# Three sets of sixteen small loads in SyncE's queue of a one-core decode block

## The chip, the cores and the metric

The kernel runs on one core of one Trainium2 chip. The metric is the device time of one launch in microseconds. Several runs are taken and their median is given; the profile is of one further execution, with the trace's clock.

## The reference

A decode step for four sequences (B = 4, one token each, D = 512). The normalized input feeds two branches whose results are added to the input:

```python
xn = layernorm(x)
out = x + A(xn, k_cache, v_cache, wq, wo) + B(xn, w1, w2, w3, w4)

# A: attention of one query against a cache, 32 heads, 4096 positions, head size 128
q = (xn @ wq) as (B, 32, 1, 128)
p = softmax(q @ k_cache^T * 128 ** -0.5)
a = (p @ v_cache) as (B, 1, 4096) @ wo

# B: a shift along the sequence, which for one token leaves only zeros, then an MLP
x1 = xn + 0
b = x1 + gelu(layernorm(x1) @ w3) @ w4
```

All is float32. `k_cache` and `v_cache` are 4 x 32 x 4096 x 128, 268 MB each. `wq` and `wo` have 8.4 MB each, `w3` and `w4` 3.7 MB each.

## The kernel before

The 128 pairs of a sequence and a head are taken in 32 groups of four (`G = 4`). For a group, keys and values are each one load of 128 partitions with 64 KB a partition, 8.4 MB. There are two key buffers (`ks`) and one value buffer (`vs`).

- VectorE loops over the groups (L320 to L337). It multiplies the keys with the query in two halves (L329), sums each product over the head size (L330), and takes the maximum (L335 to L337). After each half it raises `summed`; after the second, the key buffer is free.
- ScalarE takes the exponentials (L348) and copies results out of PSUM (L353, L355); with the last it raises `done`, and the value buffer is free.
- TensorE waits for the values (`landed`), multiplies them with the exponentials (L382), and sums over partitions (L387, L389).
- SyncE issues the loads in an order written out by hand, all through the helper `load` (its instructions have line L165) and all in one queue, q1 in the profile. First come `wq`, `w3` and the keys of group 0, then the keys of group 1, the values of group 0, and the keys of group 2 in two halves. Then, for j from 0 to 29: a wait for `summed` of group j and the keys of group j + 2 (from j = 1 on), and a wait for `done` of group j and the values of group j + 1. The last group's values go into a key buffer, and `w4` into the value buffer.
- The output weight `wo` follows in seven pieces (L288 and L292), into the last key buffer once VectorE is through with it. The first piece has half of the 32 blocks; the next have 8, 4, 2 and 1; the last block is cut in two halves. Each piece has its own semaphore (`wo_sems`), and TensorE takes up the blocks piece by piece (L419, L151, and L434 for the last block).
- The result of 4 x 512 is stored in two halves, the first by SyncE and the second by ScalarE (L441). After its store SyncE raises `bye`, on which GpSimd clears the semaphores, and SyncE waits for both stores.

The input x comes in on ScalarE's queue, q10 in the profile.

Of the kernel before, what the change touches and what calls it, by code (L numbers as in the profile page):

```python
# [88 lines left out]
def decode_block(ctx: ExitStack, tc: tile.TileContext, x, k, v, wq, wo, w3, w4, out):  # L89
    nc = tc.nc  # L90
# [14 lines left out]
    def sb(name, *shape):  # L105
        return nc.alloc_sbuf_tensor(name, [P, *shape], F32).ap()

    def bank(name):
        return nc.alloc_psum_tensor(name, [P, 4 * DH], F32).ap()
# [21 lines left out]
    rz = sb("rz", G * NJ)  # L131
    ot = sb("ot", G * NJ)

    total = bank("total")[:, 0:P]
    y = bank("y")
    pv = bank("pv")
# [7 lines left out]
    def rows(flat, j):  # L144
        n = G * S * DH
        return flat[j * n:(j + 1) * n].rearrange("(p n) -> p n", p=P)

    def blocks4(start, stop, w, m, src):
# [6 lines left out]
    wo_sems = [nc.alloc_semaphore(f"wo{n}") for n in range(7)]  # L155
    sems = {n: nc.alloc_semaphore(n) for n in (
        "x", "w3", "wq", "k0", "k1", "landed", "last", "w4", "go", "pv", "copied", "poz",
        "half0", "half1", "nm", "dve", "summed", "expd", "done", "bye", "out")}
    wo_sb = ks[LAST % 2].rearrange("p (c n) -> p c n", c=WC)
    wo_cuts = ((0, 16), (16, 24), (24, 28), (28, 30), (30, WC - 1))  # L160
    w4_sb = vs[:, :NF * D].rearrange("p (m n) -> p m n", m=NF)
    g4 = vs[:, NF * D:NF * D + 4 * 32].rearrange("p (m i) -> p m i", m=4)

    def load(o, i, sem, by, *after, queue="SP"):
        return do(queue, lambda e: e.dma_start(o, i), *after, done=(sems[sem], 16, by))  # L165
# [22 lines left out]
        out=ident, in_=ident, compare_op=ALU.not_equal, fill=1.0, base=0, pattern=[[-1, P]],  # L188
# [64 lines left out]
    for c in range(NC):  # L253
        for t in range(4):
# [22 lines left out]
    parts = [load(ks[0][:, n:n + HALF], rows(kf, 2)[:, n:n + HALF], f"half{i}", 16, (sems["summed"], i + 1))  # L277
             for i, n in enumerate((0, HALF))]
    for j in range(LAST - 1):
        if j > 0:  # L280
            load(ks[j % 2], rows(kf, j + 2), f"k{j % 2}", None, SUMMED[j])
        load(vs, rows(vf, j + 1), "landed", None, DONE[j])
# [3 lines left out]
    wo_r = wo.rearrange("(p c) n -> p c n", c=WC)  # L286
    for (c0, c1), sem in zip(wo_cuts, wo_sems):
        nc.sync.dma_start(wo_sb[:, c0:c1], wo_r[:, c0:c1]).then_inc(sem, 16)  # L288
    half = D // 2
    for n, sem in enumerate(wo_sems[-2:]):  # L290
        n *= half
        nc.sync.dma_start(wo_sb[:, WC - 1, n:n + half], wo_r[:, WC - 1, n:n + half]).then_inc(sem, 16)  # L292

    def take(engine, sem, n=1):

        engine.wait_ge(sems[sem], n)
        engine.sem_inc(sems[sem], -n)  # L297
# [11 lines left out]
    with nc.Fori(0, NJ // 2, engines=OrderedEngineSet([DVE]), head_slot={DVE: 192}) as j:  # L309
        e, n = nc.vector, 0  # L310
# [8 lines left out]
        for s in range(2):  # L319
# [14 lines left out]
            rm, nm = small[:, s, 0:1], small[:, s, 1:2]  # L334
# [68 lines left out]
    for m in range(NF):  # L403
        t, g, n = (m, g4[:, m, :], 32) if m < 4 else (m % 4, gT[:, m, :], B)
# [26 lines left out]
    for t in range(4):  # L431
# [7 lines left out]
        if t % 2:  # L439
            q = slice(P * (t - 1), P * (t + 1))  # L440
            stored = do("SP" if t < 2 else "ACT", lambda e: e.dma_start(out.rearrange("b s d -> (b s) d")[:, q], row[:, q]),  # L441
                        *moved.values(), done=(sems["out"], 16, 8 * t + 8))

    nc.sync.sem_inc(sems["bye"], 1)
    nc.scalar.sem_inc(sems["bye"], 1)
    nc.gpsimd.wait_ge(sems["bye"], 2)
# [31 lines left out]
```

## Time and profile before

| | |
|---|---|
| median of 3 runs | 1302.76 us (1302.56 to 1303.01) |
| profiled execution: span from first to last instruction | 1301.5 us; no separate time is given for this execution |
| median less this span | 1.26 us |
| TensorE matmul busy | 368.7 us (28%) |
| TensorE weight load busy | 132.8 us (10%) |
| VectorE busy | 1164.4 us (89%) |
| ScalarE busy | 93.5 us (7%) |
| GpSimd busy | 2.5 us (0%) |
| TensorE clock granted, mean | 0.622 |
| HBM read | 561.00 MB, 431 GB/s over the span |

Busy shares are taken over the whole span. In a window or a queue's line, the "share of 16 engines" is the time of that queue's packets, divided by sixteen times the length of the window; a packet is put down to the window in which it starts, so that a short window can show more than 100%. A load is one data packet for each row and, on each transfer engine that it uses, one short packet that raises the semaphore, which is called its completion here. The time "to landing" runs from the issue to the last completion.

### The profile page before, as it was taken

The page shows a single profiled execution, that of the slowest core. Times are in us where ns is not written, and L with a number is a line of the kernel's source. Part 1 is how long each engine was busy: PE and PEld are TensorE (multiplying, and loading weights), DVE is VectorE, ACT ScalarE, POOL GpSimd, SP SyncE. Part 2 cuts the span into 40 slices and gives each one's busy share as a digit, 9 for nine tenths or more (in the row PEclk, how much of TensorE's full clock was granted, in tenths as well). Part 3 has the DMA queues.
Part 4 walks back from the last instruction along what each step waited for, and adds up shares of the span by engine and source line. Part 5 has one row for each costly group of instructions (what it writes and reads, how often), then busy time and mean ns, then how long its engine had stood idle before and what let it go on. Part 6 is the DMA issues. An engine that isn't in the chain of part 4 may idle for free. (4 is left out here: it accounts for less than half of the span.)

```text
span 1301.5 us, 6687 instructions
## 1 busy us (share of the span) xinstructions
PE 368.7 (28%) x2652; PEld 132.8 (10%) x2652; DVE 1164.4 (89%) x323; ACT 93.5 (7%) x332; POOL 2.5 (0%) x14
## 2 busy tenths in 40 slices
PE   4121332321233321133331133332123332123337
PEld 2000111100011100011110011110011110001112
DVE  2599999999999999999999999999999999999990
ACT  0100000000000000000000000000000000000001
POOL 0000000000000000000000000000000000000000
PEclk9555666655666655666655566665566665566668
DMA  9999999999999999999999999999999999999998
GB/s 404 448 421 449 423 441 427 435 435 425 443 423 447 423 447 421 441 429 431 439 421 447 423 447 423 445 423 437 433 425 445 421 447 423 447 423 443 425 426 367
DMA packets 10830, 561.08 MB, mean 431 GB/s; under 512 B 1212, under 2 KB 1476, under 8 KB 1736
## 3 DMA queue, kind: packets, MB, share of 16 engines
q1 hardware_dynamic: 10808, 561.00, 99.7%
q8 instruction: 3, 0.05, 0.0%
q14 instruction: 3, 0.02, 0.0%
q10 hardware_dynamic: 16, 0.01, 0.0%
HBM read 561.00 MB, written 0.01 MB: 431 GB/s over the span
## 5 line engine op out<-in xcount | busy, mean ns | idle before, releaser
L329 DVE TENSOR_TENSOR ks<-ks,qb 128x8192 f32<-128x8192 f32 x64 | 556.3, 8692 | 63.7 <-DVEq L297 58.7
L330 DVE TENSOR_REDUCE sc<-ks 128x64 f32<-128x8192 f32 x64 | 555.9, 8686 | 2.2
L382 PE MATMUL pv<-vs,pw 128*32 128x512 f32 x1984 | 286.9, 743 | 874.9 <-PEq L297 874.9
L382 PEld LDWEIGHTS pv<-vs,pw 128*32 128x32 f32 x1984 | 79.2, 133 | 1057.9 <-issue 1057.9
L353 ACT COPY os<-pv 128x512 f32<-128x512 f32 x32 | 18.7, 585 | 827.8 <-ACTq L297 827.8
L348 ACT ACTIVATE pw<-sc,small 32x128 f32<-32x128 f32 x128 | 50.9, 398 | 278.1 <-ACTq L297 276.9
L387 PE MATMUL poz<-sel,os 128*128 128x4 f32 x256 | 32.8, 252 | 28.0 <-PEq L297 28.0
L387 PEld LDWEIGHTS poz<-sel,os 128*128 128x128 f32 x256 | 31.0, 191 | 56.1 <-issue 56.1
L348 ACT ACTIVATION_READ_ACCUMULATOR pw<-sc,small 32x1 f32 x128 | 23.5, 184 | 0.0
L436 DVE COPY os<-total 4x128 f32<-4x128 f32 x2 | 0.6, 282 | 16.2 <-PE total L434 16.2
L335 DVE TENSOR_REDUCE small<-sc 128x1 f32<-128x128 f32 x32 | 9.2, 286 | 4.7
L363 DVE RECIPROCAL rz<-oz 128x96 f32<-128x96 f32 (+1 forms) x2 | 1.1, 552 | 12.6 <-ACT oz L355 12.5
L389 PE MATMUL poz<-rs,ones 128*128 128x4 f32 x64 | 11.7, 253 | 0.0
L245 DVE STREAM_TRANSPOSE vs<-pw 128x1024 f32<-128x1024 f32 x1 | 1.2, 1245 | 10.9 <-ACT pw L244 10.9
L321 DVE STREAM_TRANSPOSE qb<-qg 128x128 f32<-128x128 f32 x32 | 10.0, 312 | 1.1
L202 DVE TENSOR_REDUCE lns<-vs 4x1 f32<-4x512 f32 x1 | 0.7, 674 | 11.3 <-DMA vs<-in_A_x_dram 11.3
L320 DVE COPY qg<-qT 128x4 f32 x32 | 5.4, 170 | 4.9 <-issue 4.9
L389 PEld LDWEIGHTS poz<-rs,ones 128*128 128x128 f32 x64 | 9.7, 192 | 0.0
L215 PE MATMUL pt<-vs,pw 4*128 4x4 f32 x16 | 4.0, 372 | 18.1 <-DVE pw L209 18.1
L419 PE MATMUL y<-ks,X 128*4 128x512 f32 x48 | 8.0, 835 | 3.5 <-DMA ks<-in_A_wo_dram 3.5
L355 ACT COPY oz<-poz 128x8 f32 x32 | 5.3, 165 | 50.8 <-ACTq L297 50.8
L382 PE MATMUL pv<-ks,pw 128*32 128x512 f32 x64 | 8.5, 692 | 0.0
(75 smaller groups left out, 74.8 us busy)
## 6 DMA issues: line engine op xcount, KB each, us to landing
ks<-in_A_k_cache_dram SPq DMA_DIRECT2D x2, 4096.0 KB, 26.9
vs<-in_B_w_dram SPq DMA_DIRECT2D x2, 3584.0 KB, 23.1
ks<-in_A_wo_dram SPq DMA_DIRECT2D x1, 4096.0 KB, 21.9
ks<-in_A_wo_dram SPq DMA_DIRECT2D x1, 2048.0 KB, 26.5
ks<-in_A_wo_dram SPq DMA_DIRECT2D x1, 1024.0 KB, 28.6
ks<-in_A_wo_dram SPq DMA_DIRECT2D x1, 512.0 KB, 29.4
ks<-in_A_k_cache_dram SPq DMA_DIRECT2D x31, 42.2
vs<-in_A_v_cache_dram SPq DMA_DIRECT2D x31, 26.8
```

The costliest lines, as they stand in the source:

```text
L320: step(e.tensor_copy(qg, pairs[:, s, bass.ds(j, 1)].rearrange("p o n -> p (o n)")))
L321: step(e.transpose(qb.rearrange("p (n m) -> p n m", m=HP), qg.unsqueeze(2).to_broadcast([P, DH // HP, HP])))
L329: step(e.tensor_tensor(out=kt, in0=kt, in1=qb.unsqueeze(1).to_broadcast([P, w, DH]), op=ALU.mult))
L330: step(e.reduce_sum(sc[s][:, c:c + w], kt, axis=AX.X))
L335: step(e.reduce_max(rm, sc[s], axis=AX.X))
L348: i = nc.scalar.activation(pw[hp, :, 4 * h:4 * h + 4], sc[s][hp, :].rearrange("p (g w) -> p g w", w=4), AF.Exp, bias=small[hp, s, 1:2], sc ...
L353: nc.scalar.copy(os, pv.rearrange("p (m d) -> p m d", m=4)).then_inc(sems["copied"], 1)
L355: nc.scalar.copy(ozs[:, s, :, bass.ds(j, 1)].rearrange("p n o h -> p n (o h)"), poz[:, 0:2 * G].rearrange("p (n h) -> p n h", n=2)).then_i ...
L382: i = nc.tensor.matmul(pv[32 * t:32 * t + 32, :], pw[:, g, :], vt[:, 4 * g:4 * g + 4, :], start=(g < 4), stop=(g >= NG - 4))
L387: nc.tensor.matmul(poz[:, 0:G], os[:, m, :], sel.rearrange("p (h m) -> p m h", m=4)[:, m, 0:G], start=(m == 0), stop=(m == 3))
L389: nc.tensor.matmul(poz[:, G:2 * G], ones.to_broadcast([P, P]), rs, start=True, stop=True).then_inc(sems["poz"], 1)
L419: i = nc.tensor.matmul(y[32 * t:32 * t + B, :], X[:, c, :], wo_sb[:, c], start=False, stop=(c >= 20))
```

## The change

A helper `ladder(n)` lets SyncE issue sixteen loads. The k-th, for k from 1 to 16, reads k rows of k + 1 numbers from `wo` (rows 32n to 32n + k, that is 8 to 68 bytes a row) into k partitions of a new tile `tiny`. Nothing reads that tile. All raise one new semaphore, `tiny`, by 16 each. The helper is called three times: ahead of the iteration j = 4 of SyncE's loop, which is right behind the issue of the values of the fifth group; behind the first piece of `wo`; and behind its last piece. Ahead of raising `bye`, SyncE waits for all 48 loads.

```diff
+    tiny = sb("tiny", 3, 152)
...
     sems = {n: nc.alloc_semaphore(n) for n in (
         "x", "w3", "wq", "k0", "k1", "landed", "last", "w4", "go", "pv", "copied", "poz",
-        "half0", "half1", "nm", "dve", "summed", "expd", "done", "bye", "out")}
+        "half0", "half1", "tiny", "nm", "dve", "summed", "expd", "done", "bye", "out")}
...
+    def ladder(n):
+
+        for k in range(1, 17):
+            at = k * (k + 1) // 2 - 1
+            nc.sync.dma_start(tiny[:k, n, at:at + k + 1], wo[32 * n:32 * n + k, 0:k + 1]).then_inc(sems["tiny"], 16)
...
     for j in range(LAST - 1):
+        if j == 4:
+            ladder(0)
         if j > 0:
             load(ks[j % 2], rows(kf, j + 2), f"k{j % 2}", None, SUMMED[j])
         load(vs, rows(vf, j + 1), "landed", None, DONE[j])
...
     for (c0, c1), sem in zip(wo_cuts, wo_sems):
         nc.sync.dma_start(wo_sb[:, c0:c1], wo_r[:, c0:c1]).then_inc(sem, 16)
+        if c0 == 0:
+            ladder(1)
     half = D // 2
     for n, sem in enumerate(wo_sems[-2:]):
         n *= half
         nc.sync.dma_start(wo_sb[:, WC - 1, n:n + half], wo_r[:, WC - 1, n:n + half]).then_inc(sem, 16)
+    ladder(2)
...
+    nc.sync.wait_ge(sems["tiny"], 3 * 16 * 16)
     nc.sync.sem_inc(sems["bye"], 1)
```

## The prediction

> **What bounds the kernel now.** I read the page's head and its transfer section first, then the costliest groups, then SyncE's own timeline, and last the end of the span in narrow windows.
>
> The page, its head and its transfer lines:
>
> ```profile
> span 1301.5 us, 6687 instructions
> DMA packets 10830, 561.08 MB, mean 431 GB/s; under 512 B 1212, under 2 KB 1476, under 8 KB 1736
> q1 hardware_dynamic: 10808, 561.00, 99.7%
> q10 hardware_dynamic: 16, 0.01, 0.0%
> L329 DVE TENSOR_TENSOR ks<-ks,qb 128x8192 f32<-128x8192 f32 x64 | 556.3, 8692 | 63.7 <-DVEq L297 58.7
> L330 DVE TENSOR_REDUCE sc<-ks 128x64 f32<-128x8192 f32 x64 | 555.9, 8686 | 2.2
> ks<-in_A_k_cache_dram SPq DMA_DIRECT2D x31, 42.2
> vs<-in_A_v_cache_dram SPq DMA_DIRECT2D x31, 26.8
> ```
>
> SyncE's queue, q1, keeps the sixteen transfer engines busy for 99.7% of the span, and it carries nearly all of the bytes. VectorE is the runner-up: a group costs it two products and two sums, 2 x 8.692 + 2 x 8.686 = 34.8 us, and small steps. It waits 58.7 us in all ahead of its products, so it is not the bound. SyncE's timeline over the whole span gives the pace (start, length, line):
>
> ```profile
> 217.63 0.33 SPq L165 DMA_DIRECT2D vs<-in_A_v_cache_dram  x1
> 233.13 0.33 SPq L165 DMA_DIRECT2D ks<-in_A_k_cache_dram  x1
> ...
> 415.96 0.33 SPq L165 DMA_DIRECT2D ks<-in_A_k_cache_dram  x1
> ...
> 1190.01 0.33 SPq L165 DMA_DIRECT2D ks<-in_A_k_cache_dram  x1
> ...
> 1267.41 2.50 SPq L288 DMA_DIRECT2D ks<-in_A_wo_dram  x5
> 1269.96 0.90 SPq L292 DMA_DIRECT2D ks<-in_A_wo_dram  x2
> 1299.93 0.35 SPq L441 DMA_DIRECT2D out_dram<-os  x1
> ```
>
> Between 415.96 and 1190.01 lie twenty groups: 774.05 / 20 = 38.70 us each, for 16.78 MB of keys and values, which is 434 GB/s. A group is sixteen rows of 64 KB for each of the sixteen engines, so 2.42 us a row. A value load alone needs half of the 38.70 us, 19.35, yet lands 26.8 us after its issue: 7.5 us of other work was queued ahead of it. For a key load it is 42.2 - 19.35 = 22.9 us. So neither issue is late; only work given to the transfer engines themselves can lengthen this stage.
>
> Do the engines advance together? Completions are the packets under 512 B, one for each engine. Four windows, 262.4 to 263.2 and 263.2 to 264.4, then 1249.4 to 1250.2 and 1250.2 to 1251.4, each around the end of one load:
>
> ```profile
> DMA packets 28, 0.92 MB, mean 1147 GB/s; under 512 B 14, under 2 KB 14, under 8 KB 14
> DMA packets 4, 0.13 MB, mean 109 GB/s; under 512 B 2, under 2 KB 2, under 8 KB 2
> ...
> DMA packets 28, 0.92 MB, mean 1147 GB/s; under 512 B 14, under 2 KB 14, under 8 KB 14
> DMA packets 4, 0.13 MB, mean 109 GB/s; under 512 B 2, under 2 KB 2, under 8 KB 2
> ```
>
> Fourteen engines finish within 0.8 us and two up to 1.2 us later, and a thousand us on it is the same. An engine that is behind stays behind by the same amount, and one that is ahead waits for nobody, as it goes on to the next queued load. A load counts as landed when its last engine is done. So a delay put on a leading engine costs nothing until it overtakes the last one; a delay of the last one passes whole into the end.
>
> The end: two steps of the chain of waits, then the output weight's later pieces (KB, us from issue to landing), then TensorE's last weight load.
>
> ```profile
> 1267.41 21.91 DMA ks<-in_A_wo_dram
> 1289.46 7.99 PE y L419 x48
> ```
>
> ```profile
> ks<-in_A_wo_dram SPq DMA_DIRECT2D x1, 2048.0 KB, 26.5
> ks<-in_A_wo_dram SPq DMA_DIRECT2D x1, 1024.0 KB, 28.6
> ks<-in_A_wo_dram SPq DMA_DIRECT2D x1, 512.0 KB, 29.4
> ks<-in_A_wo_dram SPq DMA_DIRECT2D x1, 256.0 KB, 29.2
> ks<-in_A_wo_dram SPq DMA_DIRECT2D x2, 128.0 KB, 29.0
> ```
>
> ```profile
> 1299.44 0.10 PEld L434 LDWEIGHTS total<-ks,X 128*4 128x4 f32 x4 [0.22 <-DMA ks<-in_A_wo_dram]
> ```
>
> The first piece lands at 1289.32. The last matmuls (L434) wait for the last piece, to 1299.44, so the end too hangs on the queue. The other six pieces, 4.19 MB, took 1299.44 - 1289.32 = 10.12 us; at 434 GB/s they would have taken 9.67. The 0.45 us over that pays for 6 x (8 rows + 1 completion) = 54 packets on each engine, some 8 ns each.
>
> **The change part by part.** Nothing is removed. Added are 48 small loads by SyncE, 1 + 2 + ... + 16 = 136 rows of 8 to 68 bytes in each set, one semaphore, a 1.8 KB tile, and one wait of SyncE ahead of its last signal.
>
> *How many packets, and where.* In the head's counts, 75 loads of 128 rows give 75 x 16 = 1200 completions, and the four-row input with the two four-row stores 12 more: 1212, as the line says; q10, which carries the input and one store, has 16 packets, twice four rows and four completions. A load of k rows with k below 16 thus runs on k engines, one row and one completion on each. So an engine has at most 16 rows and 16 completions of a set, 8.5 of each on average. The Trainium skill, page "DMA: Bandwidth & Descriptors", section "Why a DMA increments its semaphore by 16 and not by 1", says that such a load takes the lowest-numbered k engines; by it engine 0 has all 16 and engine 15 one; with engines drawn in turn, each would have 8 or 9 and my price below would halve. No view here numbers the engines; I take 16 as the bound either way.
>
> *Price of one.* Three windows on q10: the input's rows (2 KB, 7.2 to 8.5), its completions (9.7 to 10.9), then the store's rows and completions (1 KB, 1301.0 to 1301.2).
>
> ```profile
> q10 hardware_dynamic: 4, 0.01, 1.6%
> ...
> q10 hardware_dynamic: 4, 0.00, 0.2%
> ...
> q10 hardware_dynamic: 8, 0.00, 6.9%
> ```
>
> Shares are of sixteen engines: 1.6% of 16 x 1.3 us is 0.333 us, 83 ns a row of 2 KB. 0.2% of 16 x 1.2 is 0.038 us, some 10 ns a completion. 6.9% of 16 x 0.2 is 0.221 us; less four completions 0.181, 45 ns a row of 1 KB. From 83 and 45 the line reaches 7 ns at no bytes; I take 10 for 8 to 68 bytes. So 20 ns for a row with its completion, and 16 x 20 = 0.32 us a set on the most loaded engine. Upper end by the nearest measured row, 1 KB: 16 x 55 = 0.9 us.
>
> *First set*, behind the fifth value load (217.63). Seven issues took 2.50 + 0.90 us, about 0.5 each, and the four-row store's 0.35 is no longer than the 0.33 of a large load; sixteen take 8 us, to 226, and the next key load is issued at 233.13: 7 us of cover, and the key load could itself be 22.9 us late. Past the cover a key load would lose what its issue is late beyond that. On the engines: 0.32 us if the last engine is the most loaded, nothing if it is another. Taken: 0.2 us.
>
> *Second set*, between first and second piece. SyncE issues the second piece not at 1267.9 but 8 us later, at 1276. When do the engines need it? A window on 1287.0 to 1287.4:
>
> ```profile
> DMA packets 16, 0.13 MB, mean 328 GB/s; under 512 B 8, under 2 KB 8, under 8 KB 8
> ```
>
> Half of them complete the first piece there, so the second has some 11 us in hand. On the engines the set lies ahead of all six later pieces, and so of L434: 0 to 0.32 us, taken 0.2.
>
> *Third set*, behind the last piece. No load of the weight is behind it. SyncE is through with it at 1276 + 3.4 + 8 = 1287, before its store at 1299.93. The store stands in the same queue: the set occupies an engine 0.32 us past 1299.4, while the store is only issued at 1299.93, so it is clear. With 0.9 us it would delay the first store by about 0.3 us. The final wait stands behind the issue of that store; the set has landed by then and the store's own landing ends the kernel. Taken: 0.1 us, for the wait and the semaphore.
>
> *SyncE's instructions.* 48 more may bring one more fetch. A fetch beside the load stream looked like this (q8, 1274.4 to 1275.6):
>
> ```profile
> q8 instruction: 1, 0.02, 5.8%
> ```
>
> 5.8% of 16 x 1.2 us is 1.1 us on one engine: nothing on a leading one, up to 1.1 on the last. It may also fall otherwise than now and take as much off. Taken: nothing.
>
> Sum: 0.2 + 0.2 + 0.1 = 0.5 us, worked out against the profiled span of 1301.5 us; the median of the runs, 1302.76, is 1.26 us above that span, and I carry this over: 1303.3 us. Under 0.2% (2.6 us) counts as no change that a measurement of this kernel can tell.
>
> **The rivals.**
>
> *Small writes are dear (slower).* If a row of under 100 bytes is not a short packet but a read, a change and a write back, an engine would pay two of the 1 KB row's passages and their turnaround: 2 x 45 + 10 = 100 ns, 1.6 us a set. Two sets stand ahead of the last piece and the third delays the store by about 1 us: up to 4.2 us, 1307.0, less the lead of the loaded engines. It decides from 1.3 us a set (80 ns a load) on. For it: no row here is under 1 KB other than completions. Against: 45 and 83 ns fall in a straight line, and completions themselves, 4 bytes, take 10. The Trainium skill, page "DMA: Bandwidth & Descriptors", section "Specifications", states that below 512 B a transfer does a read-modify-write; no run here shows data that small. Chance 8%.
>
> *One after the other (slower).* If each completion held up the next load on its engine until its write is confirmed, a set would cost 16 times that. The last piece's final packets and the weight load that they release bound it (q1, 1298.9 to 1299.0):
>
> ```profile
> q1 hardware_dynamic: 2, 0.00, 3.4%
> ```
>
> From there to 1299.44 is about 0.45 us, so 7 us a set, 14 for two: 1317. Against it: the six pieces had six completions in 0.45 us of overhead together; at 0.45 each it would be 2.7. The same page's section "Anatomy of one DMA" gives about 2.0 us fixed for one DMA, as a fit for another path; 48 in series would be an estimated 96 us, 1399. The pieces here landed far closer together than that. Chance 3%.
>
> *SyncE starves the queue (slower).* If a small load took SyncE over (1287 - 1268.4) / 16 = 1.16 us, the second piece would come late and each further us would cost 16. The 0.35 us of the four-row store speaks against it. A limit on outstanding loads would act alike; the weight's seven stood queued together at 1270.9 and were issued at the same pace. Chance 3%.
>
> *Slightly faster.* The added rows or a shifted fetch could leave the last engine earlier than now by up to the 1.1 us of one fetch: 1301.7. More than 2.6 us would need faster engines, and nothing gives them fewer bytes. Chance of more than 0.2%: 2%.
>
> **How the numbers follow.** Forecast 84%: 1303.3, its own range 1302.3 to 1304.9 (nothing, to 0.9 x 2 + 0.3). Dear writes 8%, serial completions 3%, starvation 3%, faster 2%. The range reaches over the forecast's and into the dear writes: 1302.2 to 1306.0. Slower by over 0.2%: 8 + 3 + 3 = 14, of which some 2 stay below the bound, so 12%; faster 2%; within 86%.
>
> **What would show it.** Right: 272 more packets for each set, 11,646 in all or a few more, and completions with rows under 512 B at 1212 + 816 = 2028; the key loads still 38.70 us apart; the second piece issued near 1276 and L434's last load within 1 us of 1299.44; two late engines at each load's end, the gap changed by under 0.4 us after 245. Wrong: a window on one set in which sixteen engines show more than 0.1 us a load, L434 later by over 2 us, or the second piece issued after 1287.

## The result: 4.4 us slower, and the profile after

The changed kernel took 1307.16 us (median of 6 runs, 1307.10 to 1307.47) against 1302.78 us for the kernel before (6 runs, 1302.55 to 1303.03), a ratio of 1.0034 with a 95% interval of 1.0022 to 1.0046: +4.38 us. The profiled execution itself took 1307.10 us with a span of 1305.3 us.

The head of the page after:

```profile
span 1305.3 us, 6735 instructions
DMA packets 11646, 561.10 MB, mean 430 GB/s; under 512 B 2028, under 2 KB 2292, under 8 KB 2552
q1 hardware_dynamic: 11624, 561.02, 99.6%
```

The packets are the 11,646 and 2028 that were forecast. SyncE's timeline (start, length, line):

```profile
218.56 0.33 SPq L173 DMA_DIRECT2D vs<-in_A_v_cache_dram  x1
218.93 5.71 SPq L170 DMA_DIRECT2D tiny<-in_A_wo_dram  x16
233.08 0.36 SPq L173 DMA_DIRECT2D ks<-in_A_k_cache_dram  x1
...
417.29 0.33 SPq L173 DMA_DIRECT2D ks<-in_A_k_cache_dram  x1
...
1191.31 0.33 SPq L173 DMA_DIRECT2D ks<-in_A_k_cache_dram  x1
...
1269.09 5.67 SPq L170 DMA_DIRECT2D tiny<-in_A_wo_dram  x16
1274.80 2.72 SPq L298 DMA_DIRECT2D ks<-in_A_wo_dram  x4
1277.56 9.83 SPq L304 DMA_DIRECT2D ks<-in_A_wo_dram  x2
1287.43 8.91 SPq L170 DMA_DIRECT2D tiny<-in_A_wo_dram  x16
1302.60 0.27 SPq L454 DMA_DIRECT2D out_dram<-os  x1
```

The pace of the key loads is unchanged, (1191.31 - 417.29) / 20 = 38.70 us. The first set is issued well inside its cover. SyncE stands still at 1277.56, 9.83 us for two issues, which it did not do before. The store comes 2.67 us later than the 1299.93 of before. TensorE's last weight load says why:

```profile
1302.13 0.10 PEld L447 LDWEIGHTS total<-ks,X 128*4 128x4 f32 x4 [0.25 <-DMA ks<-in_A_wo_dram]
```

The last piece lets it go 2.69 us later than at 1299.44. So the sum of 4.38 us is: 2.67 us until the store is issued; from there to the end of the span 1305.3 - 1302.60 = 2.70 us instead of 1.57, 1.13 us more; and the time over the span, 1307.16 - 1305.3 = 1.86 us instead of 1.28, 0.58 us more.

Where does the 2.67 us arise? First, two windows at the end of the load that was shown before at 262.4 to 264.4, here 262.7 to 263.4 and 263.4 to 265.7:

```profile
DMA packets 15, 0.52 MB, mean 749 GB/s; under 512 B 7, under 2 KB 7, under 8 KB 7
DMA packets 24, 0.98 MB, mean 427 GB/s; under 512 B 9, under 2 KB 9, under 8 KB 9
```

Before, fourteen engines completed within 0.8 us and two up to 1.2 us later. Now seven complete within 0.7 us and the other nine are spread over 2.3 us more. The set pulled the engines apart, and the last one is later. The trace also keeps the time of each semaphore increment: the sixteen of one load were spread over 1.74 to 1.77 us in the value and key loads up to the first set, and over 2.8 us in every one behind it, at 263 us as at 1250. Second, a late engine during the first set, when nearly all others are past it: 244.52 to 244.69 and then 244.69 to 244.80.

```profile
q1 hardware_dynamic: 27, 0.00, 9.6%
...
q1 hardware_dynamic: 1, 0.07, 225.7%
```

The 27 small packets take 9.6% of 16 x 0.17 us = 0.26 us, 9.7 ns each, as the prediction priced them. But the one large row that starts behind them takes 225.7% of 16 x 0.11 us = 3.97 us, and a row takes 2.42. The price is real and does not show on the small packets: it shows as 1.55 us on the next large row. All sixteen engines together, 243.07 to 244.90:

```profile
q1 hardware_dynamic: 304, 1.06, 189.8%
```

189.8% of 16 x 1.83 us is 55.6 us. Sixteen large rows of 2.42 and 288 small packets of 9.7 ns would be 41.5. The set cost the engines 14.1 us over its packets, unevenly. The sizes of the small packets tell in the trace how many loads of the set lie ahead of each large row: the rows behind one to four last 2.42 to 2.45 us, as without the set, the row behind five 2.56 and the row behind sixteen 4.47. So about the first four cost next to nothing, and each further one costs (4.47 - 2.42) / 12 = 0.17 us.

### The profile page after: what moved, and what is told of

Same layout as the page of the kernel before. It is cut to its first block, busy times and chain, and to the rows that moved or that the text cites. A ratio compares the mean times of both kernels' runs of the same rounds, so it can differ in the third digit from the quotient of the medians.

```text
span 1305.3 us, 6735 instructions
## 1 busy us (share of the span) xinstructions
PE 363.6 (28%) x2652; PEld 131.1 (10%) x2652; DVE 1164.5 (89%) x323; ACT 93.5 (7%) x332; POOL 2.5 (0%) x14
## 2 busy tenths in 40 slices
DMA packets 11646, 561.10 MB, mean 430 GB/s; under 512 B 2028, under 2 KB 2292, under 8 KB 2552
## 5 line engine op out<-in xcount | busy, mean ns | idle before, releaser
L395 PE MATMUL pv<-vs,pw 128*32 128x512 f32 x1984 | 282.9, 734 | 879.4 <-PEq L310 879.4
```

The costliest lines, as they stand in the source:

```text
L395: i = nc.tensor.matmul(pv[32 * t:32 * t + 32, :], pw[:, g, :], vt[:, 4 * g:4 * g + 4, :], start=(g < 4), stop=(g >= NG - 4))
```

## The experiments

Three questions: which set costs what, what in a small load has the price, and when it is not paid.

**One set at a time.** Each kernel keeps one of the three calls, with the wait set to it.

```diff
 # e1_first keeps ladder(0), e2_second ladder(1), e3_third ladder(2)
-    nc.sync.wait_ge(sems["tiny"], 3 * 16 * 16)
+    nc.sync.wait_ge(sems["tiny"], 16 * 16)
```

> Only the first set, behind the fifth value load. Theory E (a small load takes some 0.15 us of each engine that it uses, most of it as a longer next large row): the last engine of each later load comes about 1.0 us later than before (gap from first to last completion 2.8 us instead of 1.7), and the end with it: +1.0 us, 1303.8. Theory S (the cost is SyncE standing still at a full queue among the weight's pieces): no change, 1302.8.

> Only the second set, between the first and the second piece of the output weight. Theory E: the last engine comes 1.3 to 1.7 us later at the last piece, +1.5 us, 1304.3. Theory S: all of the delay of the last piece, +2.7 us, 1305.5, with SyncE standing still for some 9 us at the last two pieces as it did with all three sets.

> Only the third set, behind the last piece. Theory E: the last piece lands as before, but the first half's store stands behind the set on its engines: 0.9 to 1.1 us later, and the wait for the set holds the final signal another 0.5 us: +1.5 us, 1304.3. Theory S: no change, 1302.8, as nothing of the weight is behind it.

Measured against 1302.77: 1303.93 us for the first set alone (ratio 1.0009, 1.0000 to 1.0018), 1303.88 for the second (1.0009, 1.0000 to 1.0018), 1303.25 for the third (1.0004, 0.9995 to 1.0013). That is +1.16, +1.11 and +0.48, each alone at or under the limit of what the runs tell apart. SyncE in the second and in the third:

```profile
1276.74 8.89 SPq L302 DMA_DIRECT2D ks<-in_A_wo_dram  x2
```

```profile
1270.88 21.10 SPq L170 DMA_DIRECT2D tiny<-in_A_wo_dram  x16
1299.81 0.27 SPq L450 DMA_DIRECT2D out_dram<-os  x1
```

SyncE stands still in both, 8.89 and 21.10 us, and theory S falls: the kernel with the longer stop is the cheaper one, its store is issued no later than before (1299.81 against 1299.93), and without any stop the first set costs as much as the second. For theory E the first came as expected, the second was 0.4 us cheaper, and the third much cheaper than its +1.5: alone it delays no store.

The three add up to 2.75 us, not 4.38. The leads would account for it: an engine that is ahead of the last swallows a delay once. Alone, the second set meets engines with the lead that they had before; behind the first set the lead of the loaded ones is spent. This is argued and not shown, as no run has the first two sets without the third. TensorE's last weight load with the first set alone, and with the second alone:

```profile
1300.41 0.10 PEld L444 LDWEIGHTS total<-ks,X 128*4 128x4 f32 x4 [0.23 <-DMA ks<-in_A_wo_dram]
```

```profile
1300.36 0.10 PEld L444 LDWEIGHTS total<-ks,X 128*4 128x4 f32 x4 [0.20 <-DMA ks<-in_A_wo_dram]
```

Each is about 0.95 us behind the 1299.44 of before; with all three sets it was 2.69.

**The wait.**

```diff
-    nc.sync.wait_ge(sems["tiny"], 3 * 16 * 16)
     nc.sync.sem_inc(sems["bye"], 1)
 ...
     nc.sync.sem_inc(sems["out"], -32)
+    nc.sync.wait_ge(sems["tiny"], 3 * 16 * 16)
+    nc.sync.sem_inc(sems["tiny"], -3 * 16 * 16)
```

> All three sets as in the changed kernel, but SyncE waits for the small loads at the very end, behind its wait for both stores, so that the final signal and GpSimd's clearing do not wait for them. If the wait is what makes the time exceed the span by 1.86 us instead of 1.28: 1306.6, 0.55 us under the changed kernel. If the wait costs nothing: 1307.2.

Measured: 1306.82 us (1.0031, 1.0019 to 1.0043), 0.34 us under the changed kernel, which these runs do not separate from nothing. The time over the span separates it better: it was 1.30 to 1.36 us in the six runs here, 1.80 to 1.87 us in the six of the changed kernel, and 1.28 to 1.41 us in the 28 of the kernel before. So waiting for the third set ahead of the last signal costs some 0.5 us. With the third set alone the time over the span was 1.76 us in the median, 0.43 more than before, which is nearly all of its +0.48.

**What has the price: the load or the row?** Five doses in place of the three sets, each behind the fifth to the twelfth value load, with all sixteen engines loaded alike, so that no lead hides anything.

```diff
 # p1_rows68; p3_rows512 and p5_rows1k with rows of 128 and 256 numbers
+        if n:
+            nc.sync.wait_ge(sems["tiny"], 16 * 16 * n)
+        for k in range(16):
+            p, at = 16 * (k % 8), 128 * (k // 8)
+            nc.sync.dma_start(tiny[p:p + 16, at:at + 17], wo[16 * k:16 * k + 16, 0:17]).then_inc(sems["tiny"], 16)
 # p2_one_load: the same 256 rows as one load
+        nc.sync.dma_start(tiny[:16].rearrange("p (r c) -> p r c", r=16),
+                          wo[0:256, 0:17].rearrange("(r p) c -> p r c", p=16)).then_inc(sems["tiny"], 16)
 # p4_from_sbuf: p1 with the rows read from qT
 ...
-        if j == 4:
-            ladder(0)
+        if 4 <= j < 12:
+            ladder(j - 4)
```

> Dose in place of the three sets: behind each of eight value loads (fifth to twelfth) sixteen loads of 16 rows of 68 bytes, so that every one of the sixteen engines gets 16 short rows and 16 completions each time and none has a lead to spare. Theory L (the price belongs to a load, with its completion): 16 x 0.15 = 2.4 us a set, +19 us, 1322. Theory R (the price belongs to a row under 512 bytes): the same, 1322. If the price were the 25 ns that the short packets themselves show: +3.2 us, 1306.

> The same 256 short rows of 68 bytes behind each of the eight value loads, but as one load with one completion an engine. Theory L: 0.15 us and 16 short packets of 13 ns a set, 0.35 us, +2.8 us at most, 1305.6. Theory R: 16 x 0.13 to 0.15 us a set as with sixteen loads, +17 to 19 us, 1321.

> Sixteen loads of 16 rows behind each of the eight value loads as in the first dose, but rows of 512 bytes. The bytes alone are 19 ns a row. Theory L: 2.4 us a set still, +19 to 21 us, 1322. Theory R with the bound at 512 bytes: 16 x (28 + 12) ns = 0.64 us a set, +5 us, 1308.

> The first dose (sixteen loads of 16 rows of 68 bytes behind each of eight value loads), but read from SBUF and not from HBM. If the price is the way of a short read to HBM and back, it falls to a third or less: +3 to 6 us, 1307. If it belongs to the load's handling or to the short write: +19 us as in the first dose, 1322.

> The dose of sixteen loads of 16 rows behind each of eight value loads, with rows of 1 KB. If the price of a load (some 0.163 us an engine in the dose with 68 bytes) is a pace that the bytes run under: as with 68 bytes, 1323.7 to 1325. If the bytes come on top of it: 128 x 35 ns = 4.5 us more, 1328.

| dose, eight times | us | over before (1302.73) | ratio, 95% interval |
|---|---|---|---|
| 16 loads, rows of 68 B | 1323.66 | +20.9 | 1.0161, 1.0144 to 1.0178 |
| 1 load, the same rows | 1306.29 | +3.6 | 1.0028, 1.0017 to 1.0039 |
| 16 loads, rows of 512 B | 1324.76 | +22.0 | 1.0170, 1.0153 to 1.0187 |
| 16 loads, rows of 1 KB | 1328.82 | +26.1 | 1.0210, 1.0194 to 1.0225 |
| 16 loads, 68 B, from SBUF | 1323.41 | +20.7 | 1.0157, 1.0140 to 1.0174 |

The price is the load's: 20.9 / 128 = 0.163 us each. The same rows in one load cost a sixth. Rows of 512 B come within 1.1 us of rows of 68 B, no more than their bytes (128 x 16 ns = 2.1 us), so no step shows at 512 B; and the source makes no difference that the runs can tell. Rows of 1 KB lie 5.2 us over 68 B, with 4.5 expected if the bytes come on top; their four runs lie far apart, from 1327.7 to 1332.5, so this size is rough. The same window, 243.0 to 245.3, in the first and the second dose:

```profile
q1 hardware_dynamic: 544, 1.07, 208.9%
```

```profile
q1 hardware_dynamic: 304, 1.07, 125.2%
```

Of 16 x 2.3 us these are 76.9 and 46.1 us. Less sixteen large rows (38.7) and the small packets at 9.7 ns (5.1 and 2.8), 33 us remain with sixteen loads and 4.6 with one: 2.1 and 0.3 us an engine.

**When it is not paid.** Nearly the same number of loads, in fours; then 24 loads on ScalarE's queue; then the change with each set as one load.

```diff
 # p6_fours, behind each of thirty value loads
+        for k in range(4):
+            nc.sync.dma_start(tiny[16 * k:16 * k + 16, 0:17], wo[16 * k:16 * k + 16, 0:17]).then_inc(sems["tiny"], 16)
 # p7_act_queue, ahead of ScalarE's loop; no set on SyncE
+    for k in range(24):
+        p, at = 16 * (k % 8), 32 * (k // 8)
+        nc.scalar.dma_start(tiny[p:p + 16, at:at + 17], wo[16 * k:16 * k + 16, 0:17]).then_inc(sems["tiny"], 16)
 # e5_merged, at the change's three places
+        nc.sync.dma_start(tiny[:16, n, 0:17], wo[32 * n:32 * n + 16, 0:17]).then_inc(sems["tiny"], 16)
```

> 120 loads of 16 rows of 68 bytes, nearly the 128 of the first dose, but only four at a time, behind each of thirty value loads. If every small load has a flat price of 0.163 us: +19.6 us, 1322. If an engine works some loads ahead, so that a run's first four pass unseen (in the changed kernel the engines with one to four small loads had a next large row only 0.00 to 0.03 us longer): 120 x 25 ns and 30 x 0.03 us, +4 us, 1306.6.

> 24 loads of 16 rows of 68 bytes in ScalarE's queue, issued ahead of its loop, beside the load stream of SyncE's queue; SyncE issues none. If a load holds its engine for 0.163 us whatever its queue: +3.9 us, 1306.7. If the engine prepares the two queues apart, so that a small row between two large ones costs only its packets: 24 x 25 ns, +0.6 us, 1303.4.

> The changed kernel with each set made one load of 16 rows of 68 bytes, at the same three places. If the price is by the load: three loads, each among the first four of a run, +0.1 to 0.5 us, 1303.1. If it were by the place (behind the fifth group, amid the pieces, behind them): about the changed kernel's +4.4 us, 1307.

In fours: 1307.49 us (1.0039, 1.0026 to 1.0052), +4.8 for 120 loads, 0.04 us each against 0.163 in runs of sixteen. The flat price falls: sixteen in a row pay it, four in a row hardly. On ScalarE's queue: 1303.36 (1.0005, 0.9996 to 1.0014), +0.6, as expected for packets alone, though the interval also holds no change; it excludes the +3.9. One load a set: 1302.83 (1.0000, 0.9991 to 1.0010), no difference that the runs can tell. The places are innocent. The page of the fours and, for ScalarE's queue, of the 24 loads' own issue (KB, us to landing):

```profile
q1 hardware_dynamic: 14648, 561.14, 99.7%
```

```profile
tiny<-in_A_wo_dram ACTq DMA_DIRECT2D x24, 1.1 KB, 49.1
```

The fours have 3840 packets more than before in the same queue and cost a quarter of the first dose. The 24 loads on ScalarE's queue take 49 us each to land and cost the stream next to nothing. Their rows are spread over 83 us of the trace, between the large ones, so this run does not tell whether the other queue or the wide spacing spared the price.

**Where it shows on completions.** The changed kernel's last stores tell more. Here are two windows: 1301.82 to 1303.30, between the third set's packets and the stores', and 1303.66 to 1303.87, the second store's packets:

```profile
DMA packets 0, 0.00 MB, mean 0 GB/s; under 512 B 0, under 2 KB 0, under 8 KB 0
```

```profile
q10 hardware_dynamic: 8, 0.00, 6.5%
```

The third set's packets are all out by 1301.82, and the stores' last by 1303.87, 8 packets as fast as before. Yet the span, which waits for the stores' semaphore, ends at 1305.3, 1.4 us later; before, it was 1301.5 behind packets that ended by 1301.2. So a semaphore increment can trail its packet when many were sent ahead of it. SyncE's wait for the small loads ahead of `bye` shows the same, in the changed kernel and with the third set alone (us in total, times, longest):

```profile
SPq L458 <- DMA tiny<-in_A_wo_dram: 2.0, 1, 2.0
```

```profile
SPq L454 <- DMA tiny<-in_A_wo_dram: 0.8, 1, 0.8
```

By the trace's times of the increments, the last of the small loads comes at 1304.88, 3.05 us behind the last small packet. The last ones come in step: 1304.34, 1304.52, 1304.70 and 1304.88 for small loads, then 1305.06 and 1305.23 for the stores. So increments land about 0.18 us apart, though a small load's row and completion take an engine only some 20 ns, and the step is close to the price of a load, 0.163 us. That fits a price on the completion of a load, which the next large row then has to wait for once more than a few are behind. No run took the completion away from a load, so the split between the completion and the start of a new load stays open, and so does why the first four are nearly free: in fours the last increments are as far apart (246.04, 246.21, 246.37, 246.53), while the sixteen rows behind them last 2.50 us on average.

## Why the prediction was wrong

- *What bounds the kernel*: right. The pace of 38.70 us, the cover of the first set and the place where the end hangs (L434, now L447) held.
- *Counts*: right to the packet.
- *Price of one*: this is the step that failed. It was 20 ns for a row with its completion, from the length of packets that stood alone. The packets did take that (9.7 ns each), but in a run of sixteen a load costs 0.163 us on average, and the rest shows on the row behind, 0.17 us for each load beyond about the fourth. The "upper end", 55 ns, was the length of a longer packet, and so missed it in the same way. The six pieces of the weight, with 0.45 us of overhead together, were no bound either: they move 8 rows each with every completion and are six, not sixteen.
- *First and second set*: 0.2 us each were taken; alone they measured 1.16 and 1.11, together 2.67 up to the store, and L434 came later by over 2 us, which the prediction had named as a sign of being wrong. Its mechanism, that an engine's lead swallows a delay once, fits: the spread of a load's completions grew by 1.1 us and stayed so. With the true price it would give sets that cost more together than alone; no run tests that pair by itself.
- *Third set*: taken at 0.1 with the statement that its store is clear. Its packets were clear of the store, but its completions were not: that "the set has landed by then" failed, as SyncE waited 2.0 us for it. In the changed kernel the stores landed 1.13 us later behind these completions, and the final wait added some 0.5; that is 1.6 us of the 4.38, where 0.1 was taken. Alone, the third set did not hold up the stores (1301.4 - 1299.81 = 1.6 us to the end of the span, as before) and cost only the wait.
- *SyncE*: the issue was a little faster than taken (5.67 us for sixteen, not 8), the second piece came at 1274.80. Its issue did stand still, for 9.83, 8.89 and 21.10 us. That fits the limit on outstanding loads which the prediction named, though no run shows what SyncE waited for. The stops cost nothing that the runs can tell, as the longest one stands in the cheapest of the three kernels with one set.
- *Fetches*: taken at nothing; both profiled executions have three packets on q8 and three on q14, and no run isolates them.
- *The rivals*: "dear small writes" gave up to 4.2 us and came nearest in time, for the wrong reason. It rested on rows under 512 B, and rows of 512 B and 1 KB pay the same price. The Trainium skill's page "DMA: Bandwidth & Descriptors", section "Specifications", states a read-modify-write below 512 B; no run here shows a step there. "One after the other" was right that the price is the load's and that increments land one after the other, and wrong in the size (0.163 us a load, increments 0.18 us apart, and not 0.45) and in applying it from the first load on.
- The Trainium skill's page "DMA: Bandwidth & Descriptors", section "Why a DMA increments its semaphore by 16 and not by 1", has the lowest-numbered engines take a load of few rows. This case's trace agrees that the loads are unequal: by the sizes of its packets, one engine has sixteen small loads of the first set and others fewer, down to one. Which numbers these engines have, no view here shows. So the bound of 16 loads on one engine was right.

## What to carry to other kernels

Price a small load by what it does to the transfer behind it, not by the length of its own packet: look at the next large row on the same engines. Where a queue feeds a saturated stream, put many small rows into one load, send no more than a few small loads in a row, or use another queue; in these runs 256 rows in one load cost a sixth of what they cost in 16 loads, fours cost a quarter, and 24 loads spread out on a second queue cost 0.6 us, which the runs do not tell from nothing. A delay on one of sixteen engines counts only beyond its lead, so test small delays together as well as one at a time.

## What the runs showed of the hardware that was not expected

- Runs of sixteen small loads cost 0.163 us of each engine a load, with no difference between 68 B from HBM and from SBUF, and with 512 B and 1 KB only about their bytes more; in runs of four it was 0.04 us. The row behind one to four small loads was hardly longer (2.42 to 2.45 us behind the first set, 2.50 on average in fours); each further load made it 0.17 us longer.
- Once the set was between the weight's pieces, or behind them, SyncE's issue stood still, for 9.83 and 21.10 us (the latter with the third set alone). Behind the value loads, where a count gives at most 50 packets queued on an engine (a value and a key load of 9 each, and sixteen small loads of 2), it did not.
- Semaphore increments of a run landed about 0.18 us apart and trailed the last packet by up to 3.05 us; the stores' trailed theirs by 1.4 us, where 0.3 us was seen before.
- The sixteen engines kept their distance: a load's completions were spread over 1.7 us from the 50th to the 1250th us before, and over 2.8 us for a thousand us behind one set.
